# Moving one layernorm apply, its neighbours in the queues, and one attention step in a fused Hedgehog attention and GEGLU block

## The chip, the core and the metric

The kernel runs on one core of a Trainium2 chip. The metric is the device time of one execution in microseconds (us). A core has five engines, each with its own queue of instructions that it runs in order: TensorE (PE, matmuls and weight loads), VectorE (DVE), ScalarE (ACT), GpSimd (POOL) and SyncE (SP, which here issues all DMAs). An engine that waits for a semaphore holds everything behind it in its queue.

## The reference, cut to what matters

```python
def A(x, wqkv, w_phi, wo):                       # B=1, S=2048, D=640, H=32, Dh=20
    q, k, v = split_heads(x @ wqkv)
    pq, pk = per_head(q, w_phi), per_head(k, w_phi)
    phi_q = concat(softmax(pq), softmax(-pq))     # over 20 features of a head
    phi_k = concat(softmax(pk), softmax(-pk))
    kv, z = sum_over_s(phi_k * v), sum_over_s(phi_k)
    o = (phi_q @ kv) / (phi_q @ z + 1e-6)
    return o @ wo
def B(x, w_gate, w_up, w_down):                   # F=1536
    return (gelu(x @ w_gate) * (x @ w_up)) @ w_down

h = x + A(layernorm(x), ...)
out = h + B(layernorm(h), ...)
```

Inputs and output are bf16.

## The kernel before

The 2048 rows are cut into 16 tiles of 128 rows (t = 0 to 15), and four tiles make a tile block. The weights `w_phi` are folded into the projections of k and q on the chip (`fold`), so `pk` comes directly out of `Wk2` and `pq` out of `Wq2`. Nearly the whole program is recorded in an order that is written out by hand; each engine runs its instructions in that order.

**The tile loop** (lines 442 to 486) has one unit for each t. A unit issues, in this order:

- `k_tile(t)` (line 300): ten matmuls into the PSUM tile `pk`, and two exponentials on ACT into `E`, for +pk and -pk;
- in units 10 to 14 one `fold` of the q weights: six matmuls into `wa`, and a copy into `Wq2` on ACT (line 236);
- in unit 15 four groups `q_mm(j)` and `q_exp(j)` (lines 354, 366). `QG` says which (block, column chunk) pairs, numbered 5 x block + chunk, a group holds. Pairs 0 to 4 read `LN1T` of tile block 0, pairs 5 to 9 that of tile block 1;
- in units 5, 9, 13 and 15 some `kv_tile(i)` (line 332), matmuls that add phi_k^T v of tile i into the PSUM tile `kvp`; tiles 12 to 15 follow after the loop;
- `v_mm(t + 4)`: ten matmuls into `pv`;
- `ln_ap(t + 6, on_act=True)` (line 256): the layernorm apply `ln` on ACT (`ln_act`, line 133), then a DMA transpose into `LN1T`, issued by SP;
- `v_ev(t + 4)`: ACT copies `pv` into `vS`;
- in even units up to 6 `ln_st(t + 8, t + 9)` (line 252): statistics of two tiles, four `bn_stats` and two aggregates on DVE, and then `ve`, `rstd` and two `mr` rows on POOL (lines 121 to 127); `mr` is the bias of the ACT form of the apply;
- `k_norm(t)` (line 308): on DVE the sum `sk` and the reciprocal `rs`; on POOL one half of the product `vt` (line 320), and for the tiles in `VP` = (0, 2, 4, 6, 9, 11) both halves. For the other tiles DVE does the second half between `sk` and `rs` of the next unit.

Tiles 0 and 1 went a different way at the start: their layernorm was only centred, and the factor `rstd` was applied later. So the proper `ln` of tiles 0 and 1 (`CT`), which only q needs, is made at the end of unit 10 on DVE (`ln_dve`, line 138), with a DMA transpose each. At the end of unit 9 POOL prepares `KV` and `kmask` (lines 474 to 482). In unit 13 SP issues the loads of `Wg`, `Wo` and `Wu`.

From unit 3 on, `pk`, `wa`, `pv` and `pq` share three PSUM buffers in turn (`psG`, line 445), so each waits until the one three places earlier was read.

**After the loop** `kv_mask` makes `KV`. `attn_a(t)` (line 547) multiplies phi_q of a tile with `KV` (`ab`) and copies the result to `AB`; `attn_b`, `attn_b2` and `attn_b3` divide; a transpose gives `oT`; `attn_c` multiplies with `Wo`; `attn_d`, `attn_d2` and `attn_e` make the second layernorm. `weave` (line 705) mixes these steps of later tiles into the gate/up and down units of the feed-forward part: `attn_at(t, i, offs)` puts the eight steps of tile t ahead of the units i + offs. In this part four PSUM buffers rotate among `ab`, `gu`, `po` and `pd`.

## Time and profile before

| | |
|---|---|
| time, median of three runs | 277.09 us (276.90 to 277.39) |
| the profiled execution | 277.39 us, of which the span of the core's instructions is 275.5 us |
| granted TensorE clock | 1.0 |
| busy in the span | PE 270.5, DVE 176.8, ACT 139.4, POOL 97.2 us |
| DMA | 21.37 MB, mean 78 GB/s |

In the lines of the profile "out<-in" are the program's tile names without their numbers, L338 is line 338 of the kernel, and the number in front of an engine in a timeline line is the start in us from the start of the span, followed by the time that the merged instructions took together. What stands in square brackets is how long the engine sat idle before, and what ended that. PEld are PE's weight loads, which run beside its matmuls. Matmul records overlap each other, since matmuls are pipelined and their ends are modelled. In a waits line the numbers are the time in all, how often, and the longest.

### The profile page before, as it was taken

The numbers are of one execution on the slowest core, as the hardware profiler recorded it, in microseconds if no ns is written. First come the engines' busy times: TensorE is split into PE (matmuls) and PEld (weight loads), VectorE is DVE, ScalarE is ACT, GpSimd is POOL, SyncE is SP. The second block draws the span as 40 slices with busy tenths as digits, with TensorE's granted clock in tenths as the row PEclk, the third lists the DMA queues.
The fourth block names the chain that finished last, engine by engine and source line by source line (L and its number), as shares of the span: only waits on it lengthen the run. The fifth ranks groups of instructions, "written<-read, shape, count | busy, mean of one in ns | idle before, by whom it ended". The sixth has DMA issues, their size and how long they took to land.

```text
span 275.5 us, 5930 instructions
## 1 busy us (share of the span) xinstructions
PE 270.5 (98%) x2335; PEld 174.2 (63%) x2348; DVE 176.8 (64%) x335; ACT 139.4 (51%) x239; POOL 97.2 (35%) x218
## 2 busy tenths in 40 slices
PE   8999999999999999999999999999999999999995
PEld 5777767765455887788764555675555576444574
DVE  6889999999495776675478773356866333333322
ACT  4879898869489755374552345223245510223100
POOL 4248897765202317365312553101165300000000
PEclk9999999999999999999999999999999999999999
DMA  7973526589820021316111142110123111000011
GB/s 207 194 236 61 73 53 104 80 261 393 273 87 0 4 50 35 85 49 70 32 48 48 26 69 51 38 61 2 48 47 71 26 48 50 25 0 0 0 50 48
DMA packets 42235, 21.37 MB, mean 78 GB/s; under 512 B 35040, under 2 KB 40416, under 8 KB 42208
## 3 DMA queue, kind: packets, MB, share of 16 engines
q1 hardware_dynamic: 42208, 21.01, 31.1%
q8 instruction: 18, 0.29, 0.5%
q14 instruction: 9, 0.07, 0.1%
HBM read 10.18 MB, written 2.62 MB: 46 GB/s over the span
## 4 chain that ended last, share of the span: by engine, by line
PE 72%; DVE 13%; issue 7%; SPq 4%; DMA 2%; ACT 1%; POOL 1%; DVEq 0%; ACTq 0%; POOLq 0%
PE gu L663 37%; PE pd L682 19%; PE po L603 8%; DVE sk L312 6%; PE pq L363 5%; DVE rs L316 3%; DVE stats L109 3%; PE ab L531 2%; SPq L186 2%; DMA x_sb<-in_A_x_dram 2%; POOL vt L320 1%; DVE vt L320 1%; PE tp L146 0%; ACT L666 0%; DVE mv L113 0%
## 5 line engine op out<-in xcount | busy, mean ns | idle before, releaser
L666 ACT ACTIVATE g<-gu 128x512 bf16<-128x512 f32 (+1 forms) x60 | 30.7, 512 | 68.6 <-PE gu L663 68.4
L669 DVE TENSOR_TENSOR GT<-gu,g 128x512 bf16<-128x512 f32 (+1 forms) x60 | 34.5, 580 | 47.9 <-PE gu L663 39.3
L663 PE MATMUL gu<-LN2T,Wg 128*128 128x512 bf16 (+1 forms) x291 | 61.3, 335 | 0.5
L663 PE MATMUL gu<-LN2T,Wu 128*128 128x512 bf16 (+1 forms) x300 | 61.7, 336 | 0.0
L682 PE MATMUL pd<-Wd,GT 128*128 128x320 bf16 (+2 forms) x396 | 53.5, 295 | 0.0
L682 PEld LDWEIGHTS <-GT 128*128 128x128 bf16 x396 | 37.9, 98 | 14.7 <-DVE GT L669 0.2
L663 PEld LDWEIGHTS <-Wu 128*128 128x128 bf16 x300 | 29.4, 98 | 22.6
L663 PEld LDWEIGHTS <-Wg 128*128 128x128 bf16 x300 | 28.8, 98 | 21.4
L272 PEld LDWEIGHTS <-LN1T 128*128 128x128 bf16 x290 | 27.7, 98 | 10.8 <-DMA LN1T<-ln 0.3
L685 DVE TENSOR_TENSOR y<-pd,x_sb 128x320 bf16<-128x320 f32 (+2 forms) x29 | 13.9, 480 | 29.0 <-PE pd L682 29.0
L320 POOL TENSOR_TENSOR vt<-vS,rs 128x672 bf16<-128x672 bf16 x22 | 29.1, 1344 | 9.1 <-DVE rs L316 8.8
L603 PE MATMUL po<-Wo,oT 128*128 128x320 bf16 x160 | 24.3, 299 | 0.0
L272 PE MATMUL pk<-Wk,LN1T 128*128 128x320 bf16 x160 | 24.2, 299 | 0.0
L363 PE MATMUL pq<-LN1T,Wq 128*128 128x512 bf16 x96 | 22.9, 379 | 0.2
L312 DVE TENSOR_REDUCE sk<-E 128x64 f32<-128x1280 bf16 x16 | 22.9, 1431 | 0.0
L368 ACT ACTIVATE Eq<-pq 128x1024 bf16<-128x1024 f32 (+1 forms) x26 | 20.0, 830 | 1.7 <-PE pq L363 1.7
L603 PEld LDWEIGHTS <-oT 128*128 128x128 bf16 x160 | 15.6, 98 | 7.4 <-ACT oT L147 0.5
L305 ACT ACTIVATE E<-pk 128x640 bf16<-128x640 f32 x28 | 18.2, 707 | 3.9 <-PE pk L272 3.8
L272 PE MATMUL pv<-Wv,LN1T 128*128 128x320 bf16 x130 | 19.8, 299 | 0.0
L580 DVE TENSOR_TENSOR tt<-AB,w 128x1280 bf16<-128x1280 f32 x12 | 17.9, 1488 | 1.1 <-POOL w L573 0.9
L133 ACT ACTIVATE ln<-x_sb,v,rstd 128x640 bf16<-128x640 bf16 x14 | 12.9, 920 | 10.7 <-POOL v L642 10.3
L363 PEld LDWEIGHTS <-Wq 128*128 128x128 bf16 x100 | 9.4, 98 | 10.0
(110 smaller groups left out, 294.3 us busy)
## 6 DMA issues: line engine op xcount, KB each, us to landing
out_dram<-y SPq DMA_DIRECT2D x15, 160.0 KB, 1.8
Wg<-in_B_w_gate_dram SPq DMA_DIRECT2D x1, 1920.0 KB, 7.8
Wu<-in_B_w_up_dram SPq DMA_DIRECT2D x1, 1920.0 KB, 12.5
Wd<-in_B_w_down_dram SPq DMA_DIRECT2D x1, 1920.0 KB, 8.2
x_sb<-in_A_x_dram SPq DMA_DIRECT2D x2, 640.0 KB, 6.1
Wo<-in_A_wo_dram SPq DMA_DIRECT2D x1, 800.0 KB, 9.4
x_sb<-in_A_x_dram SPq DMA_DIRECT2D x4, 160.0 KB, 2.9
Wv<-in_A_wqkv_dram SPq DMA_DIRECT2D x2, 320.0 KB, 3.9
```

Of the source, the lines that this page charges most:

```text
L272: nc.tensor.matmul(ps[:, u, 0:HD], lhsT=lnT(t, c), rhs=W[:, c, u * HD:(u + 1) * HD], start=(c == 0), stop=(c == NC - 1))
L305: nc.scalar.activation(Ek[t][:, s, :].rearrange("p (u f) -> p u f", u=2), pk[:, :, 0:HD], ACTF.Exp, scale=((lnp[t][2], nrstd[t]) if t in C ...
L312: nc.vector.reduce_sum(sk, Ek[t].rearrange("p s (h f) -> p (s h) f", f=Dh), axis=AX.X)
L320: eng.tensor_tensor(vt[:, s], vS[t % 8], rs[:, s * H:(s + 1) * H, None].to_broadcast([P, H, VC]), ALU.mult)
L363: nc.tensor.matmul(pqs[j][:, i, :], lhsT=Wq2[:, kc, c * P:(c + 1) * P], rhs=LN1T[b][:, kc, :], start=(kc == 0), stop=(kc == NC - 1))
L368: nc.scalar.activation(Eq[j][:, :, s, :], pqs[j][:, 0:len(QG[j])], ACTF.Exp, scale=(1.0, -1.0)[s])
L580: nc.vector.tensor_tensor(tt.rearrange("p s (h f) -> p s h f", f=Dh), num, w[:, :, :, None].to_broadcast([P, 2, H, Dh]), ALU.mult)
L603: nc.tensor.matmul(pos[u], lhsT=st[t][:, c, :], rhs=Wo[:, c, u * HD:(u + 1) * HD], start=(c == 0), stop=(c == NC - 1))
L663: nc.tensor.matmul(gu[i][:, 0:n], lhsT=W[:, c, f * P:(f + 1) * P], rhs=LN2T[b][:, c, a0:a1], start=(c == 0), stop=(c == NC - 1))
L666: nc.scalar.activation(g[:, 0:n], gu[0][:, 0:n], ACTF.Gelu_apprx_tanh)
L669: nc.vector.tensor_tensor(st[b, "g", f][:, a0:a1], gu[1][:, 0:n], g[:, 0:n], ALU.mult)
L682: nc.tensor.matmul(ps, lhsT=st[b, "g", f][:, tl * P:(tl + 1) * P], rhs=Wd[:, f, f0:f1], start=(f == 0), stop=(f == NF - 1))
```

## The change

- The apply of tile 0 goes from DVE in unit 10 to ACT at the end of unit 12. Its `mr`, which did not exist for this tile, is made by a new POOL instruction at the end of unit 10. The apply of tile 1 stays on DVE in unit 10. The transpose of tile 0, issued by SP, moves with the apply.
- In units 2 to 9 `ln_ap(t + 6)` goes ahead of `k_tile(t)`, so on ACT the apply stands ahead of the two exponentials instead of behind them. Unit 1 keeps the old place.
- The statistics that were made in units 2, 4 and 6 are made in units 1, 3 and 5, for the same tiles.
- The groups of q: pairs (5, 6), the first of tile block 1, now come first, and block 0 follows in the groups (0, 1), (2, 3), (4).
- `attn_a`, `attn_b`, `attn_b2` and `attn_b3` of tile 3 come one gate unit later; `attn_c` and what follows stay.
- In `attn_a` the order of the two copies is turned round for tile 4 instead of tile 5.

```diff
-    QG = ((0, 1), (2, 3), (4, 5), (6,), (7, 8), (9, 10), ...)
+    QG = ((5, 6), (0, 1), (2, 3), (4,), (7, 8), (9, 10), ...)
...
+        if t > 1 and t + 6 < NT:
+            ln_ap(t + 6, on_act=True)
         k_tile(t)
...
         if 0 < t < NT - 4:
             v_mm(t + 4)
-        if t > 0 and t + 6 < NT:
-            ln_ap(t + 6, on_act=True)
+        if t == 1:
+            ln_ap(7, on_act=True)
         if 0 < t < NT - 4:
             v_ev(t + 4)
-        if t % 2 == 0 and t + 8 < NT:
-            ln_st(t + 8, t + 9)
+        if t == 0 or t % 2 and t + 9 < NT:
+            ln_st(t + 9 - (t == 0), t + 10 - (t == 0))
         k_norm(t)
         load_T(WqT, 0, *[i for i, f in enumerate(LQ) if f == t])
         if t == 10:
-            for i in CT:
-                ln_ap(i)
+            nc.gpsimd.tensor_scalar(lnp[0][3], lnp[0][1], nrstd[0], None, op0=ALU.mult)
+            ln_ap(1)
+        if t == 12:
+            ln_ap(0, on_act=True)
...
-        for u in ((1, 0) if t in (5,) else (0, 1)):
+        for u in ((1, 0) if t in (4,) else (0, 1)):
...
-          ... + attn_at(3, 1, (1, 2, 3, 4, 9, 9, 10, 12)) + ...
+          ... + attn_at(3, 1, (2, 3, 4, 5, 9, 9, 10, 12)) + ...
```

More of the change, by code (lines that the diff above doesn't have):

```diff
@@ L50 @@
     FQ = (10, 11, 12, 13, 14)
-    QG = ((0, 1), (2, 3), (4, 5), (6,), (7, 8), (9, 10), (11, 12), (13, 14), (15,), (16,), (17,), (18,), (19,))
+    QG = ((5, 6), (0, 1), (2, 3), (4,), (7, 8), (9, 10), (11, 12), (13, 14), (15,), (16,), (17,), (18,), (19,))
     QT = (15, 15, 15, 15)
@@ L783 @@
     weave(gus(0, 0, 256) + downs(0, (0, 1)),
-          attn_at(2, 0, (-1, 0, 1, 2, 7, 7, 8, 10)) + attn_at(3, 1, (1, 2, 3, 4, 9, 9, 10, 12)) + attn_at(4, 6, SHORT2) + attn_at(5, 9, SHORT2) +
+          attn_at(2, 0, (-1, 0, 1, 2, 7, 7, 8, 10)) + attn_at(3, 1, (2, 3, 4, 5, 9, 9, 10, 12)) + attn_at(4, 6, SHORT2) + attn_at(5, 9, SHORT2) +
           attn_at(6, 13, SHORT2))
```

## The prediction, made before the changed kernel was run

> **What bounds the kernel now.** I read the page first, then the waits of TensorE (PE), then the timeline engine by engine. The page has PE busy for 98% of the span, and the waits view shows almost no wait of PE's.

> ```profile
> PE 270.5 (98%) x2335; PEld 174.2 (63%) x2348; DVE 176.8 (64%) x335; ACT 139.4 (51%) x239; POOL 97.2 (35%) x218
> ```

> ```profile
> PE kvp L338 <- POOL vt L320: 0.5, 1, 0.5
> ```

> So an edit gains only where PE stands now, and loses wherever it makes PE stand. PE stands at the end of the tile loop:

> ```profile
> 57.81 0.48 PE L227 MATMUL wa<-BD,WqT 128*128 128x140 bf16 x6
> 58.12 1.52 PE L272 MATMUL pk<-Wk,LN1T 128*128 128x320 bf16 x10
> ...
> 67.13 2.29 PE L338 MATMUL kvp<-vt,E 128*64 128x84 bf16 x110
> 69.88 0.38 PE L338 MATMUL kvp<-vt,E 128*64 128x84 bf16 x10 [0.45 <-POOL vt L320]
> ```

> 110 kvp matmuls end at 67.13 + 2.29 = 69.42, then come 0.45 us of idle. The last record lasts 0.20 us though the matmuls follow each other every 0.02 us, so PE could have gone on at 69.26: the stand is 0.62 us, until `POOL vt` of tile 15. Behind it, in the chain of waits, lies an unbroken run of VectorE (DVE) `sk` and `rs` rows. Two rows in it are long for their work:

> ```profile
> 51.52 2.17 DVE L138 TENSOR_SCALAR ln<-x_sb,mvc,rstdc 128x640 bf16<-128x640 bf16 x2
> 53.60 1.47 DVE L312 TENSOR_REDUCE sk<-E 128x64 f32<-128x1280 bf16 x1
> 55.00 1.72 DVE L320 TENSOR_TENSOR vt<-vS,rs 128x672 bf16<-128x672 bf16 x1
> 56.64 0.54 DVE L316 RECIPROCAL rs<-sk 128x64 f32<-128x64 f32 x1
> ```

> ```profile
> 49.74 2.59 POOL L320 TENSOR_TENSOR vt<-vS,rs 128x672 bf16<-128x672 bf16 x2 [1.32 <-DVE rs L316]
> 52.27 0.83 POOL L474 MEMSET KV<- 128x880 bf16 x1
> ...
> 54.69 1.32 POOL L320 TENSOR_TENSOR vt<-vS,rs 128x672 bf16<-128x672 bf16 x1
> 57.35 3.86 POOL L320 TENSOR_TENSOR vt<-vS,rs 128x672 bf16<-128x672 bf16 x3 [1.35 <-DVE rs L316]
> ```

> A DVE `vt` costs 0.85 where GpSimd (POOL) is quiet (27.82 in the DVE timeline). At 55.00 it took 1.72 and ended 0.71 after POOL's `vt` (54.69 + 1.32 = 56.01). The first `ln` ended at 53.33, 0.23 after POOL's memset of KV. So a DVE `vt` or `ln` stands until POOL's row is over, and here POOL leads: rs(9), two halves, the KV rows (2.4 us), vt(10), and only then DVE's half and rs(11).

> ScalarE (ACT) and PE in that stretch:

> ```profile
> 52.91 1.30 ACT L305 ACTIVATE E<-pk 128x640 bf16<-128x640 f32 x2 [0.54 <-PE pk L272]
> 54.09 0.70 ACT L236 CAST Wq<-wa 128x640 bf16<-128x640 f32 x1
> 54.66 1.33 ACT L305 ACTIVATE E<-pk 128x640 bf16<-128x640 f32 x2
> 55.84 0.74 ACT L236 CAST Wq<-wa 128x640 bf16<-128x640 f32 x1
> 58.01 1.30 ACT L305 ACTIVATE E<-pk 128x640 bf16<-128x640 f32 x2 [1.43 <-PE pk L272]
> ```

> ACT seems to have 1.43 us to spare before 58.01. Three PSUM buffers rotate here: wa(14), at 57.81 on PE, writes where pk(13) lay, so it needs E(13) (54.66 + 1.33 = 55.99); pk(15) at 58.12 needs the Wq copy of unit 13 (ends 56.58).

> **Tile 0's apply to ACT.** *DVE:* one `ln` leaves. Alone it is 0.43 us, in place 1.82. But the DVE half of vt(10) stood until POOL's 56.01 anyway and would stand longer, so rs(11) does not come earlier: gain 0. A bound from the other side: were DVE the leader, 0.43 to 1.82 earlier, of which PE could use 0.62. *POOL:* a 1-element row (`mr` of tile 0, 0.26 like the other `mr` rows) stands behind vt(10), so it ends no earlier than 56.01 + 0.26 = 56.27. *ACT:* ln(0), 0.92 (any `ln` row of ACT in the loop), is queued between the Wq copy of unit 12 (ends 54.79) and E(13), and waits for that POOL row. Behind it stand E(13), the copy, E(14). So with POOL at its old times: ln 56.31 to 57.23, E(13) 57.13 (ACT rows overlap by 0.10) to 58.46; wa(14) at 58.49 instead of 57.81, 0.68 late. The copy after E(13) ends 0.64 later at 59.10, while wa(14) takes 0.31: 0.3 more before pk(15). In all PE is 0.98 late.

> **Applies ahead of E, statistics a unit earlier.** The statistics of two tiles move from units 2, 4, 6 to units 1, 3, 5. On POOL their four rows now stand ahead of the odd tile's `vt`, not behind it:

> ```profile
> 21.00 0.23 POOL L121 TENSOR_SCALAR ve<-mv 128x2 f32<-128x2 f32 x1 [0.55 <-DVE mv L113]
> 21.32 0.71 POOL L122 TENSOR_TENSOR rstd<-ve,nhalf 128x2 f32<-128x2 f32 x1
> 22.12 0.50 POOL L127 TENSOR_SCALAR mr<-mv,rstd 128x1 f32<-128x1 f32 x2
> 23.01 3.86 POOL L320 TENSOR_TENSOR vt<-vS,rs 128x672 bf16<-128x672 bf16 x3 [0.38 <-DVE rs L316]
> ```

> These rows span 21.00 to 22.63, 1.63 us. From the end of one even rs to the next, POOL then needs 0.16 (rs at 22.85 to 23.01) + 2.58 (two halves) + 1.63 + 1.31 (odd half) = 5.68; DVE's half of the odd tile, due 0.6 earlier, stands until then, and adds 0.71 plus 0.46 for rs: 6.85. Before, the even rs rows ended at 22.85, 29.13, 35.47 and 41.82: 18.97 for three rounds. Now 3 x 6.85 = 20.55, 1.58 later. Bounds: 0, if POOL's small rows fit into gaps; 1.95, with 0.1 of start-up ahead of the statistics and the odd half. I take 1.58, as every row of it is in the trace. After unit 6 the order is as before, so the delay stays until POOL's vt(10), and moves the `mr` row, E(13) and wa(14) with it: PE 0.98 + 1.58 = 2.56 late.

> ln ahead of E delays E by at most 0.92 in units 2 to 9. Its DVE reader sk comes 2.6 to 3.9 later (E(8) ends 40.78, sk starts 43.74), and the PSUM buffer of pk(8) is taken by the pv matmuls at 43.91: cost 0; uncovered, up to 0.92 once. In return the transposes start earlier; the weight load that waited 0.33 for LN1T at 39.44 no longer does. That gain, some 0.16 on PE, lies before wa(14)'s new wait and is lost in it.

> **q order, SP.** Group (5,6) reads only tiles 4 to 7, long in LN1T. ln(0) would end near 58.8, its transpose lands 2.6 later at 61.4; group (0,1) starts after (5,6), 2.2 + 2.6 later than 59.48, near 64.2. Covered; (0,1) in front would have been due at 62, still after it. On SP the transpose of tile 0 now waits for ACT, and Wg, Wo, Wu stand behind it: from 55.97 to about 60, 4 us. Wo (9.4 to land) is read at 79.3, Wg (7.8) at 90.1, Wu (12.5) after that. Cost 0; without that cover up to 4.

> **phi_q@KV of tile 3.** At 92.96 PE's `gu` started when the first GT row (92.48, 0.42) freed its buffer; PE was free at 92.85. A gate unit in between removes that 0.11. Tile 3's oT is then ready about 1.1 later, near 103.2, and read at 104.42. Gain 0.11; bounds -0.11 and, if that margin is used up, +0.5. The u order of tiles 4 and 5 swaps two ACT copies of 0.75 whose buffers are not due: 0.

> [...] At 51.52 `ln` was already waiting when POOL's vt ended at 52.33, yet the memset right behind went first. By this row POOL's `mr` goes ahead of the waiting vt half, as summed. [...]

> **The sum.** The last kvp: PE arrives at 69.26 + 2.56 = 71.82. POOL's vt(15) ended at 69.82 and is later by 1.58 + 0.26 (DVE's vt(10) behind the `mr` row): 71.66, just in time, so the old stand is gone. Start 71.82 instead of 69.88: +1.94. Less 0.11: +1.83. The profiled run took 277.39 us (span 275.5 and 1.9 around it), so 279.2 by it; it is the slowest of three, 0.3 over their median 277.09, so I predict 278.9.

> **Rivals.** *A, POOL is not late:* the rounds keep their 6.3 us, only the `mr` row holds ACT. PE is 0.98 late at 70.24, less 0.62 and 0.11: +0.25, 277.3. For it: POOL is busy for only 22.3 of the 25 us from 20 to 45, so there is room. Against: the room is behind rs waits, not between the four rows. *B, faster:* DVE sheds its `ln`, vt(15) comes 0.62 earlier, PE never stands: -0.62 - 0.11 = -0.73, 276.4. It decides if the `mr` row is written by 55.6 (57.8 less 1.33 for E(13) and 0.92 for ln); in the old trace the row ahead of it ended at 56.01. *C, DVE's half goes ahead of the `mr` row:* +0.71, and rounds at the upper bound, +0.37: 280.0.

> **How the numbers follow.** A difference under 0.2% (0.55 us) is about what a measurement of this kernel can't tell from none. Forecast 0.66, C 0.16 (both slower), A 0.10 (same), B 0.08 (faster). Slower 0.82. The range 277.4 to 280.0 runs from just above A to C; it leaves out B, about A's lower half and little above.

> **What would show it.** Right: ACT's row for ln(0) begins near 57.9 after a wait of some 3 us for POOL; PE stands before wa of unit 14 for about 2.3 and before pk(15) for 0.3; the wait kvp <- POOL vt is gone or small; even rs rows 6.8 apart; PE dense afterwards, with no wait at the third gate unit. Wrong: PE without a stand between 57 and 62, or ln(0) starting before 55.7; new waits of po for oT or of PE for Wo or Wg.

## The result and the profile after

The changed kernel takes 280.25 us (median of 6 executions, 279.72 to 281.51) where the kernel before takes 277.0 (276.82 to 277.39): 1.0117 times, 95% interval 1.0099 to 1.0135. The forecast was 278.9, with a range up to 280.0. The direction held and the place held; the price was 1.35 us short.

The six executions fall into two groups, and the granted TensorE clock that each lists says which: two show 0.993 or 0.994 over the span and take 281.22 and 281.51, four show 0.999 or 1.0 and take 279.72 to 280.53. The profiled execution is the one of 281.51 us (span 279.4, and 2.1 around it), so it belongs to the longer group. On the page PE is as full as before; the row under it shows two slices in which the clock was not full, and a slice is 7 us.

```profile
PE 272.8 (98%) x2348; PEld 174.6 (62%) x2348; DVE 176.6 (63%) x334; ACT 139.8 (50%) x240; POOL 96.2 (34%) x219
...
PEclk9999999988999999999999999999999999999999
```

In the view of waits (us in total, times, longest), the wait of kvp for POOL's vt is gone. In its place stand two that form one chain: ACT's ln(0) waits for the `mr` row of tile 0 (here `mrc`), and PE's wa(14) for the E behind it.

```profile
ACT ln L133 <- POOL mrc L472: 3.4, 1, 3.4
...
PE wa L227 <- ACT E L305: 2.4, 1, 2.4
```

PE's timeline at that place (start, duration, and in brackets the idle time before the row):

```profile
56.66 1.53 PE L272 MATMUL pk<-Wk,LN1T 128*128 128x320 bf16 x10
60.57 0.47 PE L227 MATMUL wa<-BD,WqT 128*128 128x140 bf16 x6 [2.39 <-ACT E L305]
61.16 2.83 PE L272 MATMUL pk<-Wk,LN1T 128*128 128x320 bf16 x10
63.77 8.06 PE L363 MATMUL pq<-LN1T,Wq 128*128 128x512 bf16 x35
71.76 2.48 PE L338 MATMUL kvp<-vt,E 128*64 128x84 bf16 x120
```

The first and the third row are the same ten matmuls of 320 columns. The first take 1.53 us, those after the stand 2.83. From start to start the last matmul ahead of the stand and wa(14) are 2.55 us further apart than the matmul lasts; ahead of pk(15) 0.27 more are lost. All 120 kvp matmuls then run without a pause.

The windows of 1 us (sum, PE busy and its matmuls, granted clock, DMA share, GB/s) name the second loss. The clock is full while PE stands, goes to 0.50 from about 61.05, half a microsecond after PE resumed, and is back at about 64.5:

```profile
60.00:61.00 1.00, 0.43 (x6) 1.00 0.45 91
61.00:62.00 1.00, 0.89 (x5) 0.52 0.74 94
62.00:63.00 1.00, 1.00 (x6) 0.50 0.69 89
63.00:64.00 1.00, 1.00 (x5) 0.50 0.96 326
64.00:65.00 1.00, 1.00 (x5) 0.77 1.02 402
```

3.4 us at half rate lose 1.7; as PE still stood ahead of pk(15) in the first 0.1 of them, 1.6 are lost by the starts of the matmuls. So the spans compare like this: stand 2.55 + 0.27, spell of half rate 1.6, together 4.42; less what went away, kvp's stand 0.62, the weight load that waited at 39.4 (0.15) and the third gate unit (0.10), together 0.87; and 0.37 at the start, by which PE is already late at 15 us; in the waits view after, PE's `pv` waits there for the first transfer of Wv. 4.42 - 0.87 + 0.37 = 3.92; the spans differ by 279.4 - 275.5 = 3.9.

Why the `mr` row came at 58.39 and not at the 57.85 of the forecast is seen in two timelines, DVE's and POOL's:

```profile
54.69 1.47 DVE L312 TENSOR_REDUCE sk<-E 128x64 f32<-128x1280 bf16 x1
56.08 0.84 DVE L320 TENSOR_TENSOR vt<-vS,rs 128x672 bf16<-128x672 bf16 x1
```

```profile
56.12 1.98 POOL L320 TENSOR_TENSOR vt<-vS,rs 128x672 bf16<-128x672 bf16 x1
58.08 0.31 POOL L472 TENSOR_SCALAR mrc<-mvc,nrstd 128x1 f32<-128x1 f32 x1
```

Before, POOL's half of vt(10) led (54.69, 1.32) and DVE's stood. Now DVE has one ln less, starts its half 0.04 us ahead, and it is POOL's half that stands and takes 1.98, with the `mr` row behind it.

### The profile page after: what moved, and what is told of

Same layout as the page of the kernel before. It is cut to its first block, busy times and chain, and to the rows that moved or that the text cites. A ratio compares the mean times of both kernels' runs of the same rounds, so it can differ in the third digit from the quotient of the medians.

```text
span 279.4 us, 5942 instructions
## 1 busy us (share of the span) xinstructions
PE 272.8 (98%) x2348; PEld 174.6 (62%) x2348; DVE 176.6 (63%) x334; ACT 139.8 (50%) x240; POOL 96.2 (34%) x219
## 3 DMA queue, kind: packets, MB, share of 16 engines
HBM read 10.18 MB, written 2.62 MB: 46 GB/s over the span
## 4 chain that ended last, share of the span: by engine, by line
PE 79%; DVE 12%; issue 3%; POOL 2%; DMA 2%; ACT 1%; SPq 1%; DVEq 0%; POOLq 0%
PE gu L666 37%; PE pd L685 19%; PE pq L363 8%; PE po L606 8%; DVE sk L312 4%; DVE stats L109 3%; PE ab L534 3%; DVE rs L316 2%; DMA Wv<-in_A_wqkv_dram 2%; POOL vt L320 1%; PE pv L288 1%; PE pk L272 1%; PE kvp L338 1%; PE tp L146 1%; DVE vt L320 1%
## 5 line engine op out<-in xcount | busy, mean ns | idle before, releaser
L272 PEld LDWEIGHTS <-LN1T 128*128 128x128 bf16 x290 | 28.3, 99 | 11.4 <-issue 0.2
L320 POOL TENSOR_TENSOR vt<-vS,rs 128x672 bf16<-128x672 bf16 x22 | 29.9, 1375 | 10.9 <-DVE rs L316 9.6
L272 PE MATMUL pk<-Wk,LN1T 128*128 128x320 bf16 x160 | 25.5, 310 | 0.1
L312 DVE TENSOR_REDUCE sk<-E 128x64 f32<-128x1280 bf16 x16 | 22.9, 1433 | 1.2 <-ACT E L305 1.2
L272 PE MATMUL pv<-Wv,LN1T 128*128 128x320 bf16 x130 | 19.8, 299 | 0.0
L305 ACT ACTIVATE E<-pk 128x640 bf16<-128x640 f32 x28 | 18.3, 715 | 2.8 <-PE pk L272 2.8
```

The source lines that it names most:

```text
L272: nc.tensor.matmul(ps[:, u, 0:HD], lhsT=lnT(t, c), rhs=W[:, c, u * HD:(u + 1) * HD], start=(c == 0), stop=(c == NC - 1))
L305: nc.scalar.activation(Ek[t][:, s, :].rearrange("p (u f) -> p u f", u=2), pk[:, :, 0:HD], ACTF.Exp, scale=((lnp[t][2], nrstd[t]) if t in C ...
L312: nc.vector.reduce_sum(sk, Ek[t].rearrange("p s (h f) -> p (s h) f", f=Dh), axis=AX.X)
L320: eng.tensor_tensor(vt[:, s], vS[t % 8], rs[:, s * H:(s + 1) * H, None].to_broadcast([P, H, VC]), ALU.mult)
```

## Experiments

Theory 1 after this reading: the loss is the wait of ln(0) for a late POOL row, PE's stand behind it, and after the stand a spell of half rate. Rivals: the later statistics cost by themselves (2), the q order, the SP queue or tile 3's step cost something (3), the half rate has nothing to do with the stand (4). The runs below fall into three groups, each on a chip of its own, beside runs of the kernel before on the same chip. The medians of these were 277.60, 277.41 and 277.48, and they spread by 1.5 to 1.8 us, so ratios are compared, not microseconds across groups.

**The row early, the statistics back, both, the stand filled** (first chip).

e1: the `mr` row of tile 0 issued in unit 7.

```
-        if t == 10:
+        if t == 7:
             nc.gpsimd.tensor_scalar(lnp[0][3], lnp[0][1], nrstd[0], None, op0=ALU.mult)
+        if t == 10:
             ln_ap(1)
```

> The changed kernel with one row moved: POOL's 1-element mr row of tile 0 is issued in unit 7 and no longer behind vt(10). Theory 1 (the loss is ACT's ln(0) waiting 3.4 us for that row, PE's stand of 2.55 us behind it, and a spell of half-rate matmuls after the stand): ln(0) starts right behind the Wq copy, PE does not stand before wa(14), and pk(15)'s ten matmuls follow each other every 0.136 us, not 0.267. The rounds are still later, so POOL's vt(15) ends about 1.0 later than before (70.82 against 69.82) and kvp waits for it: 277.0 + 1.0 - 0.1 = 277.9. Rival 2 (the later statistics are what costs, the row matters little): over 279. Rival 3 (q order, SP queue or tile 3 cost something after the loop): over 279 with no stand before wa(14).

Measured: 278.55, ratio 1.0031 (1.0016 to 1.0047), clock 0.999 to 1.0 in all nine executions. No stand before wa(14), pk(15) at full rate; ln(0) starts at 54.52, without a wait. The rounds still take 6.81 to 6.95, and in the waits view kvp now stands twice for vt, its last part starting at 70.90, as expected:

```profile
PE kvp L338 <- POOL vt L320: 0.8, 1, 0.8
PE kvp L338 <- DVE vt L320: 0.6, 1, 0.6
```

One row of 0.3 us, moved, gives back some three quarters of the loss; the rest is rival 2's.

e2: statistics where they were.

```
-        if t == 0 or t % 2 and t + 9 < NT:
-            ln_st(t + 9 - (t == 0), t + 10 - (t == 0))
+        if t % 2 == 0 and t + 8 < NT:
+            ln_st(t + 8, t + 9)
```

> The changed kernel with the statistics back in units 0, 2, 4 and 6, behind the odd... even tile's place as before; the mr row of tile 0 still stands behind vt(10). Theory 1: the three rounds take 6.3 us again, the row ends near 56.3 to 56.9, PE stands 0.7 to 1.0 us before wa(14) and 0.3 before pk(15), too short for a half-rate spell; with the old kvp stand of 0.62 gone: 277.3, at most 277.8. Rival 2 (statistics cost most): 276.9 or less. Rival 3 (the row's wait holds PE 2.5 us whatever the rounds do): 279 or more.

Measured: 278.59, ratio 1.0041 (1.0024 to 1.0059), clock 0.998 to 1.0 in all twelve executions. The rounds take 6.28 to 6.35 again, and the stand is 0.74 + 0.27. That this is near the 0.68 + 0.3 that the prediction gives for POOL at its old times is chance: the `mr` row ends 34.10 after the first rs, 0.68 later than at POOL's old times (56.27 - 22.85 = 33.42), as DVE's half is ahead of it here too, and PE comes to wa(14) 0.59 later on the same count. By its ratio the kernel is some 0.8 us slower than expected: PE now stands 0.89 at 36.9, pv waiting for E.

e3: both edits.

> Both: mr row of tile 0 in unit 7, statistics in units 0, 2, 4 and 6. What is left of the change is ln(0) on ACT, the applies ahead of k's exponentials, the q order and tile 3's step. Theory 1: no stand before wa(14), rounds of 6.3 us; DVE has one ln less, so vt(15) comes a little earlier: between 276.4 (kvp's stand of 0.62 and the 0.11 gone) and 277.0. Rival 3 (something behind the loop costs): over 277.5.

Measured: 278.05, ratio 1.0009 (0.9995 to 1.0022): above the expectation of 0.998 to 1.0, though the interval reaches into it. The stand before wa(14) and that of kvp are gone, but pv waits as in e2 (0.91 from start to start). ACT's timeline shows what is ahead of E there:

```profile
35.22 0.92 ACT L133 ACTIVATE ln<-x_sb,mr,rstd 128x640 bf16<-128x640 bf16 x1 [1.06 <-POOL mr L127]
```

With the old statistics the apply waits for its own `mr` row, and E now stands behind it. So the statistics a unit earlier are needed for the applies ahead of E, and are what makes the rounds longer.

e4: 44 short matmuls ahead of wa(14), which nothing reads.

```
+        if t == 14:
+            for i in range(44):
+                nc.tensor.matmul(kvp[:, i % 2, 420:512], lhsT=ones[:, 0:P], rhs=ones[:, 0:92],
+                                 start=False, stop=False, skip_group_check=True)
         if t in FQ:
```

> The changed kernel as it is, with 44 added matmuls of 92 columns (about 0.04 us each, 1.8 us in all) on PE ahead of wa(14), into a part of kvp's banks that nothing reads. They fill most of PE's stand and wait for nothing. Theory 1 with the clock term: PE resumes at the same moment, and the half-rate spell (pk(15) at 0.267 us a matmul, some 1.6 us lost) is gone in every execution: all near 279.7, clock 0.999 or 1.0, none above 280.3. Rival 4 (the half rate has another cause, or the spell is no loss): times spread from 279.7 to 281.5 as those of the changed kernel, median 280.2, with half-rate spells still there. If the added matmuls outlast the stand: some 0.3 more.

Measured: 280.47 (279.71 to 281.7), ratio 1.0104 (1.008 to 1.0128), clock 1.0 in all six. No spell, as expected, but the times spread, against the expectation, so by itself this was inconclusive. In the profiled execution the DVE and POOL chain began late (first rs at 23.79, against 22.56 in the changed kernel's profile), so the `mr` row ended at 59.60 and 1.40 of stand were left behind the added matmuls.

**The race, the good parts alone** (second chip).

e5: the changed kernel again.

> The changed kernel once more, unchanged, as the yardstick for the three beside it and to see how often the half-rate spell comes. All theories: 1.011 to 1.013 of before. Theory 1 with the clock term: some executions show a granted clock near 0.993 and are about 1.5 us longer than those at 0.999 to 1.0; the kernel with the filled stand had 1.0 in all six. If no execution here falls under 0.998 the spell is rarer than the first six runs let it seem (2 of 6).

Measured: 281.41, ratio 1.0143 (1.0122 to 1.0164), clock 0.993 or 0.994 in all five. In the profile: stand 3.03 + 0.27, then a clock of 0.50 from 61.66 to 65.07.

e6: DVE held back by one row.

```
+        if t == 11:
+            pad = small(p1, [P, 2 * H], "pad", 1)
+            nc.vector.reciprocal(pad, sk)
         if t - 1 in todo:
             todo.pop(t - 1)()
```

> The changed kernel with one row added on DVE: a reciprocal of 64 columns (0.54 us) between sk(11) and DVE's half of vt(10); its result is not used. In the changed kernel's profile DVE's half started at 56.08 and POOL's half at 56.12, and POOL's then took 1.98 us instead of 1.31, with the mr row right behind it. Theory 5 (DVE, with one ln less, now wins this race by 0.04 us, and that makes the mr row and PE's stand 0.67 later): with DVE held back POOL's half takes 1.31, the mr row ends 0.67 earlier, PE's stand shrinks by 0.67, and the kernel is 0.6 to 0.7 us FASTER for the added row. Rival (the order of the two halves does not matter, POOL's row is long for another reason): same time, or slower by up to 0.54.

Measured: 281.34, ratio 1.0145 (1.0121 to 1.0168), the same as e5; clock 0.994 or less in all five. The expectation failed, and how is the most useful line of the study. POOL's half did go first and took 1.32; but then the `mr` row took 0.91:

```profile
56.02 1.32 POOL L323 TENSOR_TENSOR vt<-vS,rs 128x672 bf16<-128x672 bf16 x1
57.31 0.91 POOL L475 TENSOR_SCALAR mrc<-mvc,nrstd 128x1 f32<-128x1 f32 x1
```

```profile
56.56 1.48 DVE L323 TENSOR_TENSOR vt<-vS,rs 128x672 bf16<-128x672 bf16 x1
```

DVE's half, waiting since 56.56, ran between the two POOL rows (57.34 to 58.05), and `mr` was over only after it, at 58.23 (58.21 in e5). In the profile after, DVE's half went first (56.08), in e6 POOL's (56.02); both times the other engine's half was next, and the `mr` row was over only behind both (58.39 in the profile after).

e7: from the kernel before, only ln(0) on ACT, the q order, tile 3's step and the order of the two copies in `attn_a`, with the `mr` row in unit 7. The edit in the loop:

```
         if t == 10:
-            for i in CT:
-                ln_ap(i)
+            ln_ap(1)
+        if t == 12:
+            ln_ap(0, on_act=True)
+        if t == 7:
+            nc.gpsimd.tensor_scalar(lnp[0][3], lnp[0][1], nrstd[0], None, op0=ALU.mult)
```

> The kernel before with only these parts of the change: ln(0) on ACT, the q order and tile 3's step; and with the mr row issued in unit 7. Statistics and applies stay where they were before. Theory 6 (two parts of the change are good, but hidden by the others: DVE's chain ends 0.68 earlier without the ln, so kvp's stand of 0.62 goes; applies ahead of k's exponentials with the old statistics cost PE 0.9 us at 36.3): 276.3 where before is 277.0, ratio 0.9965 to 0.998, no PE wait over 0.3 after 16 us. Rival (DVE's ln was hidden and its removal brings nothing): ratio 0.999 to 1.001, with the wait kvp <- POOL vt of 0.5 still there.

Measured: 276.89, ratio 0.9982 (0.997 to 0.9994), just above the 0.9965 to 0.998 that was expected: faster than both kernels. All 120 kvp matmuls follow each other:

```profile
67.21 2.48 PE L338 MATMUL kvp<-vt,E 128*64 128x84 bf16 x120
```

From the first rs to the end of POOL's vt(15) the chain takes 46.26 us (22.53 to 68.79), before 46.97 (22.85 to 69.82): without its ln, DVE's chain is 0.71 shorter.

e8: from the kernel before, only the q order, tile 3's step and the order of the two copies.

> The kernel before with only the q order (second tile block in front) and tile 3's step a unit later. Theories 1 and 6: neither lies on the path, the third gate unit no longer waits for GT: 0 to -0.2 us, ratio 0.999 to 1.0. Rival 3 (one of these two costs): ratio over 1.002.

Measured: 277.4, ratio 0.9996 (0.9981 to 1.0011). For the q order and tile 3's step rival 3 is out. The SP queue is not tested here, as ln(0) stays on DVE; in the profile after, no row of PE waits for Wo, Wg or Wu.

**Statistics alone, the row one place earlier, the spell** (third chip).

e9: from the kernel before, only the statistics and the applies ahead of E.

> The kernel before with only the statistics a unit earlier and the applies ahead of k's exponentials; tile 0's and tile 1's applies both stay on DVE. Theory 7 (the three rounds take 6.9 us instead of 6.3 and nothing gives that back): the even rs rows come 1.75 later after three rounds, POOL's vt(15) with them, and kvp's stand grows from 0.62 to 2.3: 1.75 less 0.16 (the wait at 39.4) slower, ratio 1.0055 to 1.006 without a half-rate spell after the stand, 1.011 to 1.012 with one (clock near 0.994), since the stand is almost as long as that of the changed kernel, at another place. Rival 2 (the rounds' delay is absorbed, as POOL has room): ratio 1.000 to 1.002.

Measured: 278.94, ratio 1.0057 (1.0037 to 1.0077), as theory 7 says. Rounds of 6.90, 6.95 and 6.80; PE now waits three times, twice in kvp and once where theory 7 had no wait, ahead of pq's first group, which in this kernel still reads block 0, with the late applies of tiles 0 and 1:

```profile
PE kvp L338 <- POOL vt L320: 0.8, 1, 0.8
PE kvp L338 <- DVE vt L320: 0.7, 1, 0.7
PE pq L363 <- DMA LN1T<-ln: 0.6, 1, 0.6
```

From start to start these stands are 0.97, 0.84 and 0.72. With matmuls between them they brought no spell: clock 0.999 to 1.0 in all eight. So rival 2 holds beside theory 1: the later rounds cost some 1.6 us by themselves (by the ratio).

e10: the `mr` row directly ahead of POOL's vt(10).

```
         if t == 10:
-            nc.gpsimd.tensor_scalar(lnp[0][3], lnp[0][1], nrstd[0], None, op0=ALU.mult)
             ln_ap(1)
...
             nc.gpsimd.tensor_copy(KV[:, :, 1, :, 0], kmask)
+            nc.gpsimd.tensor_scalar(lnp[0][3], lnp[0][1], nrstd[0], None, op0=ALU.mult)
```

> The changed kernel with POOL's mr row of tile 0 one place earlier: ahead of vt(10) instead of behind it. Theory 1: the row ends near 56.3 instead of 58.2 to 58.4, ln(0) and E(13) follow 1.9 earlier, PE stands 1.1 before wa(14) instead of 3.0 (and 0.3 before pk(15)), too short for a half-rate spell: clock 0.999 to 1.0 in all executions, about 3.0 to 3.4 faster than the changed kernel beside it, ratio to before 1.003 to 1.005. Rival 2 (the later statistics are most of the loss): ratio over 1.008.

Measured: 279.15, ratio 1.0049 (1.003 to 1.0069), clock 1.0 in all seven: the ratio is at the end of what was expected, but the gain against the changed kernel (e11, below) is 1.5 and not 3.0 to 3.4. The stand was 2.04 and not 1.1, as DVE's half was again first, at 56.93, and took its 0.84:

```profile
56.98 0.97 POOL L485 TENSOR_SCALAR mrc<-mvc,nrstd 128x1 f32<-128x1 f32 x1
```

e11 and e12: the changed kernel, and that of e4, on one chip.

> The changed kernel, unchanged, as the yardstick for the two beside it. Theory 1 with the clock term: ratio to before 1.011 to 1.015, executions with a clock of 0.993 to 0.994 some 1.6 us longer than those at 0.999 to 1.0.

> The changed kernel with the 44 short matmuls in PE's stand (1.8 us of work that nothing reads), once more, now on the same chip as the changed kernel. Theory 1 with the clock term: ends 1.5 us earlier than those executions of the changed kernel that show a clock of 0.994, and shows 0.999 to 1.0 itself. Rival 4 (the spell costs nothing, what PE loses there it would have waited anyway): within 0.3 us of the changed kernel at whatever clock.

Measured: e11 280.62, ratio 1.0122 (1.0085 to 1.016). Three executions at clock 1.0 take 279.74, 280.23 and 280.35; two at 0.993 and 0.994 take 280.88 and 281.43; one at 0.988, twice the usual loss of clock, takes 283.51. e12: 279.96 (279.56 to 280.59), ratio 1.0087 (1.0065 to 1.0109), clock 0.999 or 1.0 in all six. It equals the executions of e11 that kept the clock, and is shorter than those that did not by 0.92, 1.47 and 3.55 us.

The profiled execution of e11 kept its clock, and makes a clean pair with the profile after. The stand is as long (2.62 + 0.27), the ten matmuls behind it take 1.52:

```profile
60.39 0.47 PE L227 MATMUL wa<-BD,WqT 128*128 128x140 bf16 x6 [2.46 <-ACT E L305]
60.98 1.52 PE L272 MATMUL pk<-Wk,LN1T 128*128 128x320 bf16 x10
```

and its span is 277.6, 1.8 shorter than that of the profile after (0.26 of it at the start). In e12 the stand is full of work but for 0.6:

```profile
57.70 2.09 PE L455 MATMUL kvp<-const-bfloat16-1.0 128*128 128x92 bf16 x44
60.21 0.48 PE L227 MATMUL wa<-BD,WqT 128*128 128x140 bf16 x6 [0.42 <-ACT E L305]
```

Counted over all groups: of 17 executions of the changed kernel 10 show a clock of 0.994 or less; with the stand filled, none of 12; in e1, e2, e3 and e7 to e10, whose stands are shorter, none of 72 (lowest 0.998). That the spell follows from the stand is thereby shown, and rival 4 is out. Why one execution has it and the next, with as long a stand, has not, is taken up in the last section.

## Why the prediction was right and wrong

*What held.* The place and the order: ACT's ln(0), E(13), wa(14), pk(15), with 0.27 for the second pause (forecast 0.3). The rounds: 1.72 over three of them (20.69 against 18.97) where 1.58 was summed; e9 alone 1.68. From the end of the `mr` row to wa(14): 2.19, forecast 2.22. ln ahead of E cost nothing in the changed kernel, and e2 and e3 show the uncovered price, 0.89 and 0.91, next to the bound of 0.92. The q order and tile 3's step: no price (e8); the SP queue: no wait of PE's for a weight behind it in the profile after.

*The first step that failed: the moment of the `mr` row, 0.8 too early.* The sum put its end at 56.27 + 1.58 = 57.85, which is 35.00 after the first rs. In the three profiles of the changed kernel it ends 35.83, 35.82 and 35.79 after it, in the two with the stand filled 35.80. Of the 0.8, 0.14 are the rounds. The rest, some 0.7, is DVE's half of vt(10), which the prediction put behind the `mr` row on the strength of one row (the memset that overtook a waiting ln at 52.3). It goes ahead, in e6 literally as rival C told it, elsewhere because DVE wins the race for vt(10). The profile of before held rows nearer to the case, which were not weighed: a DVE half of vt that ran just as POOL came to an `mr` row.

```profile
27.82 0.85 DVE L320 TENSOR_TENSOR vt<-vS,rs 128x672 bf16<-128x672 bf16 x1
```

```profile
28.07 0.96 POOL L127 TENSOR_SCALAR mr<-mv,rstd 128x1 f32<-128x1 f32 x2
```

Of these two `mr` rows the first took 0.72 and the second 0.26; the same happens at 34.40 (0.74) and 40.61 (0.88). So the DVE row at 27.82 was not one with a quiet POOL, as the prediction read it: POOL stood behind it. Rival C had this order, at +0.71; the runs side with it here, while the memset's row (0.83 at 52.27, with `ln` waiting since 51.52) remains the other way round and unexplained.

*The same race hid a second error.* "DVE loses one ln: gain 0" was argued from POOL leading. By e7, DVE's chain is 0.71 shorter without the ln: rival B's mechanism exists. The late `mr` row kept it from showing in the changed kernel, and where the row came early but the rounds stayed late (e1), kvp still waited.

*The term that was missing: the clock.* The sum let PE go on at its old rate after the stand. Three cases, with their prices: forecast 278.9; with 0.7 for DVE's half 279.6; the executions of the first measurement that kept their clock took 279.72, 279.83, 279.98 and 280.53. The spell adds 1.6 to some, and their share (2 of these 6) lifts the median to 280.25, past the range, whose upper end had DVE's half in it but no spell; without the 1.6 in those two the median would be some 279.9 (an estimate), just inside it. Nothing in the profile of before showed this price at that place, but it had a trace of it: the first warm-up matmuls of 512 columns start 0.427 us apart there, twice the 0.216 of later ones. The clock row of the page reads full there only because that trace has no clock record before 6.63 us.

*A small remainder.* Kernels with ln(0) on ACT spend 2.0 to 2.2 us outside the span (one execution of e6: 1.8), those without it (before, e8, e9) 1.8 to 1.9. These 0.2 us are not explained.

## What to carry to other kernels

A tiny row decides by its place in its queue: before a step goes to another engine, look up which row produces its operand, and what stands ahead of that row on its own engine and on the engine whose rows hold it up (here DVE's for POOL's: 0.91 us for 0.31 in e6). Price a stand of PE as long as the one here (2.55 us in the profile after) at more than its length, as the matmuls behind it may run at half rate: it was some 1.6 us more here, and 10 of 17 executions of the changed kernel show the lower clock. And when a change of many parts loses, try its parts: here the apply on the other engine, with the q order and tile 3's step, was worth 0.5 us once the row that it needs came early.

## What the runs showed of the hardware

After stands of 2.55, 3.03 and 3.07 us (the profile after, e5, e6), PE ran at half its clock for 3.41 us (61.04 to 64.45, 61.66 to 65.07 and 61.58 to 64.99), beginning not when it stopped nor when it resumed, but 0.5 to 1.3 us after; the stand of 2.62 us in the profile of e11 had no such spell behind it, nor did any of the seven executions of e10 show one (clock 1.0; the stand is 2.04 in its profile).

In e6 two rows of POOL that stood back to back did not keep DVE out: a DVE `vt` that waited from 56.56 on ran between POOL's `vt` (to 57.34) and the one-element `mr` row, which took 0.91 us where it took 0.31 in the profile after.
